# Attention by split transforms, then an ELU mixture layer: w_out in 4 KB packets with renumbered hidden units, and five reorderings beside it

## The chip, the cores and the metric

The kernel runs on one core of one Trainium2 chip. The metric is the device time of one execution in microseconds (us). A time is given as the median of several executions, and beside it stands one profiled execution, whose trace all rows come from. In the rows PE is TensorE (PEld its weight loads), DVE is VectorE, ACT is ScalarE, POOL is GpSimd and SP is SyncE, which here only issues transfers. A "q" behind the name (SPq, POOLq) is the queue of an engine.

## What is computed

```python
# x (8, 3008, 256); w_r, w_i (256, 256); b_r, b_i (256)
X = np.fft.rfft(x, axis=1)
Yr = Xr @ w_r - Xi @ w_i + b_r
Yi = Xr @ w_i + Xi @ w_r + b_i
lam = 0.01
Yr = np.sign(Yr) * np.maximum(np.abs(Yr) - lam, 0.0)
Yi = np.sign(Yi) * np.maximum(np.abs(Yi) - lam, 0.0)
y = np.fft.irfft(Yr + 1j * Yi, n=3008, axis=1)
# y as 24064 rows of 256; w_in (256, 2048); w_out (2048, 256)
h = y @ w_in
g = np.where(h > 0.0, h, np.exp(np.minimum(h, 0.0)) - 1.0)
out = g @ w_out
```

The 2048 columns of w_in and the 2048 rows of w_out are the hidden units. The function between them works on each unit alone.

## The kernel before

**The stages.** The sequence of 3008 is taken as 47 x 64, so that the transforms become products with small constant matrices. For each of the eight batches the work runs through five stages. A (`unit_A`, L186 and L194) does one half of the forward transform, X (`unit_X`, L242) the other half, M (`unit_M`; `first_M` and its helpers in the first batch, L292 to L392) the product with w_r and w_i, the bias and the soft threshold, B (`unit_B`, L448; `split_B`, L497, in the first batch) one half of the way back, and Y (`first_Y`, `split_Y`, L598; L612 later) the rest. Behind them comes the mixture layer in blocks of 512 rows: `front` (L1112) multiplies by w_in into `hps`, ScalarE takes exp (L1124), GpSimd clips (L1163), VectorE adds the linear part (`gT`, L1153), and `back` (L1184) multiplies by w_out into `ps_o`. Eight pairs of 128 hidden units make a block, 16 groups `ft` in all.

**Between the stages** data change their layout by transfers, nearly all on SyncE's queue. In the first batch A goes straight to its place in Z (L200); later it goes through `DA` in HBM. Y is turned by `by_part` into `Yx` (L428; four DMAs per call, two column parts c by two halves s), B's result goes to `DB` in HBM (L516) and comes back as `Bs` (`load_Bs`, L479). x comes in by `load_x` (L121) in three pieces per batch on GpSimd's queue.

**The order** of the instructions on each engine is the order in which the program text issues them (`manual_schedule`). An engine carries out its own list in that order and stops at an instruction whose input, or whose place to write, isn't ready. SyncE's issues take turns on eight semaphores, so that each issue also waits for the transfer eight issues before it.

**The head.** `busy` is set to ones (L621), and `idle_pe` (L628) multiplies it by itself in fp32, into a PSUM bank that nobody reads, while PE has nothing else: first two products of 512 columns and one of 256, later three and one more behind stage A (L932). Meanwhile GpSimd and VectorE make the angles, ScalarE takes their sine into `r1` (L755) and writes the first batch's weights of stage A from it, scaled by a column of plus or minus one: `M1d` (L761, four operations of 32 elements per partition) and `M1c` (L769, four more). Then ScalarE clears Z (L692) and copies A's results out of PSUM (L150).

**The weights of the mixture layer.** `load_w_in(q)` brings a quarter of w_in's columns on SyncE's queue (L952); `scale_w_in` (L962) multiplies them by 2/S and writes them as bf16 into `w_in_s`. VectorE does quarters 0 to 2, in two operations each, and GpSimd quarter 3 in four. `load_w_out(hh)` brings half of w_out on GpSimd's queue (L957) in rows of 256 floats, 1 KB each: partition p of group t holds hidden unit 128 t + p. 

**The first batch's sequence** stands written out (before the main loop). The parts that matter:

```python
    fB(3)
    load_w_in(2)
    first_M(5, 1, True)
...
    fB(5)
    let_go()
    load_Bs(0, 0, 16 * NT)
    load_w_in(3)
...
    load_w_out(0)
    load_x(1, 2)
    load_w_out(1)
```

`load_x(1, 2)` brings the last third of the second batch's x into the buffer that the first batch's stage A has read by then.

Of the kernel before, what the change touches and what calls it, by code (L numbers as in the profile page):

```python
# [9 lines left out]
AF = mybir.ActivationFunctionType  # L10
BF16 = mybir.dt.bfloat16
F32 = mybir.dt.float32
F32R = mybir.dt.float32r
# [7 lines left out]
N2 = 64  # L21
# [3 lines left out]
NS = 32  # L25
# [4 lines left out]
def kernel(  # L30
# [11 lines left out]
    nc = tc.nc  # L42
    P = nc.NUM_PARTITIONS
# [6 lines left out]
    NFT = DFF // P  # L50
# [13 lines left out]
    w_in_s = constp.tile([P, 2, DFF], BF16, name="w_in_s")  # L64
    w_out_r = constp.tile([P, NFT, E], F32R, name="w_out_r")
# [47 lines left out]
    def load_x(b, ci, m0=0, m1=8):  # L113

        src = bass.AP(
            tensor=x.tensor,
            offset=x.offset + (b * S + 8 * ci + m0) * D,
            ap=[[N1 * D, N2], [(NJ - 1) * D, 2], [D, m1 - m0], [1, D]],
        )
        dst = xts[ci][:, m0:m1, :]  # L120
        nc.gpsimd.dma_start(dst, src.bitcast(F32R))  # L121

    def unit_ps(name, alone):
        if alone:
            return pre2.tile([P, 2, 512], F32, name=name, tag="pre2")
        return last_banks("psF").tile([P, 2, 512], F32, name=name, tag="fps")
# [19 lines left out]
    def evac(dst, src, on_dve):  # L146
        if on_dve:
            nc.vector.tensor_copy(dst, src)  # L148
        else:
            nc.scalar.copy(dst, src)  # L150
# [223 lines left out]
    def begin_M(q, i, pool=begin, tag="begin"):  # L374

        begun[q, i] = ps = pool.tile([P, 2 * D], F32, name=tag, tag=tag)
        nc.tensor.matmul(ps[:], lhsT=busy[:, 0:P], rhs=bias_p[:], start=True, stop=False)
# [45 lines left out]

    def by_part(dst, of):

        for c in range(2):
            for s in range(2):
                nc.sync.dma_start(dst[c * N2 : c * N2 + N2, :, s, :], of(c, s))  # L428

    def turn_M3():  # L430
# [7 lines left out]
    def unit_B(b, v, alone=False, on_dve=False, all_dve=False):  # L438
        if (b, v // 2) not in Bz_of:
            t = "A" if alone and v == 0 else "Bz"  # L440
            Bz_of[b, v // 2] = wk2.tile([P, 8, D], BF16, name=t, tag=t)
            if b not in DB_of:
                DB_of[b] = dram.tile([K1, P, D], BF16, name="DB", tag="DB")
        Bz, Yx = Bz_of[b, v // 2], Yx_of.pop((b, v))
        ps = unit_ps("bps", alone)
        for pp in range(2):
            for s in range(2):
                nc.tensor.matmul(  # L448
                    ps[:, s, pp * D : pp * D + D], lhsT=M3x[:, 2 * v + pp, s, :],
                    rhs=Yx[:, pp, s, :], start=True, stop=True,  # L450
                )
        o = 4 * (v % 2)
        Bv = Bz[:, o : o + 4, :].rearrange("p (q s) d -> p s q d", s=2)
        psv = ps[:].rearrange("p s (q d) -> p s q d", d=D)
        if on_dve:
            nc.scalar.copy(Bv[:, :, 0], psv[:, :, 0])
            nc.vector.tensor_copy(Bv[:, :, 1], psv[:, :, 1])
        else:
            evac(Bv, psv, all_dve)
        if alone:  # L460
            k0 = 4 * v
            nc.sync.dma_start(
                DB_of[b][k0 : k0 + 4].rearrange("k p d -> p k d"), Bz[:, o : o + 4, :]
            )
        elif b == 1 and v > 1:
            nc.sync.dma_start(
                DB_of[b][4 * v : 4 * v + 4].rearrange("k p d -> p k d"), Bz[:, o : o + 4, :]
            )
        elif v % 2:
            k0 = 8 * (v // 2)  # L470
            nc.sync.dma_start(DB_of[b][k0 : k0 + 8].rearrange("k p d -> p k d"), Bz[:])

    def load_Bs(b, w, r0=0, cut=4 * K1):

        Bs = wk4.tile([4 * K1, 8, D], BF16, name="Bs", tag="Bs")
        dv = DB_of[b].rearrange("k (c h m) d -> (k c h) m d", c=2, h=2)
        for r, e in ((r0, cut), (cut, 4 * K1)):
            if r < e:
                nc.sync.dma_start(Bs[r:e], dv[r:e, 8 * w : 8 * w + 8, :])  # L479
        Bs_of[b, w] = Bs  # L480
# [139 lines left out]
    busy = constp.tile([P, 512], BF16, name="busy")  # L620
    nc.vector.memset(busy[:], 1.0)  # L621
    ips = [pre1.tile([P, 512], F32, name="ips", tag="mps1")]

    def idle_pe(n, k=2):

        ones = busy[:].bitcast(F32)
        for _ in range(n):
            nc.tensor.matmul(  # L628
                ips[-1][:].rearrange("p (a b) -> p a b", a=2)[:, 0:k], lhsT=ones[:, 0:P],
                rhs=ones.unsqueeze(1).to_broadcast([P, k, 256]), start=True, stop=True,  # L630
            )

    bias_p = wk4.tile([P, 2 * D], BF16, name="bias_p", tag="Bs")
    idle_pe(2)
    idle_pe(1, 1)
    xts = []
    for ci in range(3):
        xt = constp.tile([P, 8, D], F32R, name=f"xt{ci}")
# [1 line left out]
    with tc.tile_pool(name="stagep", bufs=1) as stagep:  # L640
        M1c = stagep.tile([P, 2, 3 * N2], F32R, name="M1c")
        M1d = stagep.tile([P, 4, 7 * NS], F32R, name="M1d")
# [5 lines left out]
        def col(eng, src, s1, op0, s2=None, op1=None, n=1, dt=F32):  # L648
            t = stagep.tile([P, n], dt, name=f"c{len(cols)}")
            cols.append(t)  # L650
            if op1 is None:
                eng.tensor_scalar(t[:], src[:], s1, None, op0)
            else:
                eng.tensor_scalar(t[:], src[:], s1, s2, op0, op1)
            return t

        def mix(eng, a, sc, b, op0, op1, n=1):
            t = stagep.tile([P, n], F32, name=f"c{len(cols)}")
            cols.append(t)
            eng.scalar_tensor_tensor(t[:], a[:], sc, b[:], op0, op1)  # L660
            return t
# [20 lines left out]
        def row(name, shape):  # L682
            return stagep.tile(shape, F32, name=name)
# [48 lines left out]
        for e in range(2):  # L732
            b3 = 1024 - 15 * e
            lo = slice(N2 * e, N2 * e + NS)
            hi = slice(N2 * e + NS, N2 * e + 2 * NS)
# [14 lines left out]
        r1 = row("r1", [P, 2 * NS])  # L750
# [4 lines left out]
        nc.scalar.activation(r1[:], v1[:], AF.Sin, bias=0.0, scale=TURN / 4.0)  # L755
        c1 = mix(dve, qcol, -2.0, pcol, ALU.mult, ALU.add)
        c0 = col(dve, c1, -1.0, ALU.mult, 1.0, ALU.add)
        for h, c in enumerate((c0, c1)):
            for q in range(2):
                o = 3 * NS + 16 * h + 8 * q  # L760
                nc.scalar.activation(  # L761
                    M1d[:, :, o : o + 8],
                    r1[:, NS * q : NS * q + NS].rearrange("p (b a) -> p a b", a=4),
                    AF.Copy, scale=c[:],
                )
        r1v = r1[:].rearrange("p (q b a) -> p q a b", q=2, a=2)
        for h, c in enumerate((c0, c1)):
            for q in range(2):
                nc.scalar.activation(  # L769
                    M1c[:, :, N2 + NS * h : N2 + NS * h + NS].rearrange(  # L770
                        "p a (q b) -> p q a b", q=2
                    )[:, q],
                    r1v[:, q], AF.Copy, scale=c[:],
                )
        for h in range(2):
            clear_Z(h)
# [150 lines left out]
        pool.tensor_copy(wcat_r[:, :, D : 2 * D], w_i_f[:])  # L927
        load_x(1, 1)
        pool.tensor_scalar(idm[:], prow, pcol[:], None, ALU.is_equal)
        for q, i in ((3, 0), (3, 1)):  # L930
            begin_M(q, i)
        idle_pe(3)  # L932
# [7 lines left out]
    M3.append(late2.tile([P, K1 // 2, P], BF16, name="M3", tag="osb"))  # L940

    w_in_v = moe_w_in.rearrange("(c p) f -> p c f", p=P)
    w_out_v = moe_w_out.rearrange("(t p) e -> p t e", p=P).bitcast(F32R)
    FQ = DFF // 4
    w_in_f = []

    def load_w_in(q):
        if q < 3:
            wf = late3.tile([P, 2, FQ], F32, name="w_in_f", tag="Et")
        else:  # L950
            wf = late2.tile([P, 2, FQ], F32, name="w_in_f", tag="osb")
        nc.sync.dma_start(wf[:], w_in_v[:, :, q * FQ : q * FQ + FQ])  # L952
        w_in_f.append(wf)

    def load_w_out(hh):
        hf = slice(hh * NFT // 2, (hh + 1) * NFT // 2)
        nc.gpsimd.dma_start(w_out_r[:, hf, :], w_out_v[:, hf, :])  # L957

    def scale_w_in(q, on_dve, c, part=None):
        lo, hi = (0, FQ) if part is None else (part * FQ // 2, part * FQ // 2 + FQ // 2)  # L960
        eng = nc.vector if on_dve else nc.gpsimd
        eng.tensor_scalar(  # L962
            w_in_s[:, c, q * FQ + lo : q * FQ + hi], w_in_f[q][:, c, lo:hi],
            2.0 / S, None, ALU.mult,
        )

# [6 lines left out]
    def fB(v):  # L973
        split_B(v, two_banks(pre2, "pre2"), (False, False))()
# [35 lines left out]
    first_M(5, 0, False)  # L1010
    begin_M(5, 1, pre1, "mps1")
    fB(3)
    load_w_in(2)
    first_M(5, 1, True)
    for c in range(2):
        scale_w_in(0, True, c)
# [5 lines left out]
    fB(5)  # L1022
    let_go()
    load_Bs(0, 0, 16 * NT)
    load_w_in(3)
    first_M(1, 0, False)
    first_M(1, 1, True)
# [7 lines left out]
            M4v[:, :, h], r4[0 : 2 * NR], w[0 : 2 * NR], None, ALU.mult  # L1035
        )
    load_w_out(0)
    load_x(1, 2)
    load_w_out(1)
    first.close()  # L1040
    lateB, chain, chain2, lateA = (
# [9 lines left out]
    rest_1, store_1, _ = split_B(1, two_banks(lateB, "lateB"), (True, True), True)  # L1051
# [257 lines left out]
    for i in range(n + LAG):  # L1309
# [4 lines left out]
        if early_h:  # L1314
            h, on_act = early_h, False
        elif i < n:
# [16 lines left out]
            h = front(i, third, on_act)  # L1333
# [52 lines left out]
```

## Time and profile before

| | us |
|---|---|
| executions | 874.69, 875.59, 875.5 |
| their median | 875.5 |
| profiled execution | 875.34 |
| its span | 873.6 |
| mean granted TensorE clock | 0.999 of full |

The span is the time from the first to the last instruction in the trace; the execution's own time is longer by what lies around it. How the rows read:

- A row of waits: engine, output and line of what waited, what ended the wait, then us in total, how many times, the longest.
- A row of the chain of waits: start and length in us, then the engine and line, or the transfer, that the end of the execution hung on at that time.
- A row of the timeline: start, busy time of the group, engine, line, operation, out<-in with partitions x elements, count, and in brackets the idle time before the group with what ended it.
- A row of transfers in a stretch: packets, megabytes, rate, and how many packets are small; or for one queue its packets, megabytes and the time that they took as a share of 16 DMA engines. q0 carries GpSimd's transfers, q1 SyncE's.
- A row of a stretch A:B in the table by stage: its length, then busy us (and instructions) of PE, PEld, DVE, ACT, POOL, then the granted clock, the busy share of the DMA engines and the GB/s.
- A row of a tile's view: line, engine, operation and count, least/median/largest ns of one, the first and last start in us, the shapes. "DMA to landing" is the time from a transfer's issue to its end.

### The profile page before, as it was taken

The page shows a single profiled execution, that of the slowest core. Times are in us where ns is not written, and L with a number is a line of the kernel's source. Part 1 is how long each engine was busy: PE and PEld are TensorE (multiplying, and loading weights), DVE is VectorE, ACT ScalarE, POOL GpSimd, SP SyncE. Part 2 cuts the span into 40 slices and gives each one's busy share as a digit, 9 for nine tenths or more (in the row PEclk, how much of TensorE's full clock was granted, in tenths as well). Part 3 has the DMA queues.
Part 4 walks back from the last instruction along what each step waited for, and adds up shares of the span by engine and source line. Part 5 has one row for each costly group of instructions (what it writes and reads, how often), then busy time and mean ns, then how long its engine had stood idle before and what let it go on. Part 6 is the DMA issues. An engine that isn't in the chain of part 4 may idle for free.

```text
span 873.6 us, 18529 instructions
## 1 busy us (share of the span) xinstructions
PE 861.2 (99%) x6760; PEld 674.9 (77%) x6760; DVE 665.9 (76%) x1104; ACT 714.7 (82%) x1258; POOL 586.9 (67%) x859
## 2 busy tenths in 40 slices
PE   8999999999999999999999999999999999999997
PEld 5567677877788877887779787788777878787776
DVE  8788778687776976768867787777777677788775
ACT  8778788888978889798887988879887888876664
POOL 8651640898757886588856888459874697734664
PEclk9999999999999999999999999999999999999999
DMA  8698337542484324743355442653337313250111
GB/s 246 226 302 242 110 97 205 171 141 78 122 242 126 92 74 143 219 140 104 95 173 174 138 110 73 205 154 125 99 87 214 100 37 86 73 146 25 38 37 49
DMA packets 115724, 116.11 MB, mean 133 GB/s; under 512 B 11552, under 2 KB 106272, under 8 KB 112272
## 3 DMA queue, kind: packets, MB, share of 16 engines
q1 hardware_dynamic: 109376, 87.40, 35.5%
q0 software_dynamic: 5968, 27.26, 9.7%
q8 instruction: 53, 0.87, 0.4%
q14 instruction: 39, 0.32, 0.1%
q10 hardware_dynamic: 288, 0.26, 0.1%
HBM read 53.28 MB, written 48.23 MB: 116 GB/s over the span
## 4 chain that ended last, share of the span: by engine, by line
PE 91%; DMA 3%; POOL 2%; DVE 2%; issue 1%; ACT 0%; SPq 0%; DVEq 0%; POOLq 0%
PE ps_o L1184 38%; PE hps L1112 33%; PE mps L334 5%; PE xps L242 3%; PE mps L1112 2%; PE yps L612 2%; PE bps L448 2%; PE aps L194 2%; PE mps L292 2%; DMA DB<-A 1%; POOL Y L350 1%; PE aps L186 1%; DMA xt<-in_x_dram 1%; DMA yb<-in_w_i_dram 1%; POOL yb L346 0%
## 5 line engine op out<-in xcount | busy, mean ns | idle before, releaser
L1153 DVE SCALAR_TENSOR_TENSOR gT<-Et,hps 128x512 fp32r<-128x512 f32 x630 | 403.0, 683 | 136.3 <-POOL Et L1163 126.3
L1184 PE MATMUL ps_o<-w_out_r,gT 128*128 128x256 f32 x3008 | 477.4, 301 | 0.8 <-DVE A L148 0.8
L1184 PEld LDWEIGHTS ps_o<-w_out_r,gT 128*128 128x128 f32 x3008 | 404.3, 189 | 49.1 <-DVE A L148 1.1
L1163 POOL TENSOR_SCALAR Et<-Et 128x512 f32<-128x512 f32 x482 | 287.0, 615 | 210.2 <-ACT Et L1124 208.9
L1112 PE MATMUL hps<-yT,w_in_s 128*128 128x512 bf16 (+7 forms) x1620 | 366.1, 353 | 0.2
L1124 ACT ACTIVATE Et<-hps 128x512 f32<-128x512 f32 x514 | 282.5, 609 | 42.4 <-PE hps L1112 39.2
L1112 PEld LDWEIGHTS <-w_in_s 128*128 128x128 bf16 x1728 | 144.0, 98 | 103.9 <-issue 11.9
L1122 ACT ACTIVATE Et<-hps 128x512 f32<-128x512 f32 x192 | 104.5, 597 | 42.0 <-PE hps L1112 41.6
L1127 ACT ACTIVATE Et<-Et 128x512 f32<-128x512 f32 x192 | 110.5, 632 | 0.0
L350 POOL TENSOR_TENSOR Y<-yb,clip 128x512 bf16<-128x512 f32 x72 | 92.7, 1288 | 6.0
L346 POOL TENSOR_TENSOR yb<-yb,bias_bc 128x256 f32<-128x256 f32 x72 | 53.1, 738 | 11.3 <-DVE yb L341 11.3
L150 ACT CAST XT<-xps 128x768 bf16<-128x768 f32 x57 | 45.8, 804 | 16.7 <-PE xps L242 16.6
L341 DVE TENSOR_TENSOR yb<-mps,yb 128x512 f32<-128x512 f32 x72 | 49.8, 692 | 7.2
L150 ACT CAST yT<-yps 128x752 bf16<-128x752 f32 x56 | 44.1, 787 | 13.7 <-PE yps L612 13.5
L1155 DVE SCALAR_TENSOR_TENSOR gT<-hps,Et 128x512 fp32r<-128x512 f32 x78 | 50.2, 686 | 3.3
L349 POOL TENSOR_SCALAR clip<-yb 128x512 f32<-128x512 f32 x72 | 44.2, 613 | 6.3
L150 ACT CAST A<-aps 128x1024 bf16<-128x1024 f32 x40 | 40.6, 1018 | 7.2 <-PE aps L194 4.9
L150 ACT CAST Bz<-bps 128x1024 bf16<-128x1024 f32 x41 | 41.6, 1014 | 5.3 <-PE bps L448 5.0
L340 DVE TENSOR_TENSOR yb<-mps,bias_bc 128x256 f32<-128x256 f32 x72 | 30.5, 424 | 17.5 <-PE mps L334 15.7
L334 PE MATMUL mps<-wcat_s,XT 128*128 128x256 bf16 x288 | 43.2, 273 | 0.0
L1196 DVE COPY osb<-ps_o 128x512 f32<-128x512 f32 x46 | 31.7, 690 | 5.4 <-PE ps_o L1184 3.4
L260 POOL TENSOR_TENSOR XS<-XT 128x512 bf16<-128x512 bf16 x30 | 34.1, 1158 | 2.4 <-ACT XT L150 1.4
(209 smaller groups left out, 666.2 us busy)
## 6 DMA issues: line engine op xcount, KB each, us to landing
xt<-in_x_dram POOLq DMA_DIRECT2D x21, 1024.0 KB, 5.3
out_dram<-osb SPq DMA_DIRECT2D x158, 128.0 KB
Bs<-DB SPq DMA_DIRECT2D x30, 384.0 KB
Yx<-Y SPq DMA_DIRECT2D x168, 64.0 KB
DA<-A SPq DMA_DIRECT2D x19, 512.0 KB
DB<-Bz SPq DMA_DIRECT2D x19, 512.0 KB
Z<-DA SPq DMA_DIRECT2D x21, 384.0 KB
xt<-in_x_dram POOLq DMA_DIRECT2D x6, 512.0 KB, 5.9
```

Of the source, the lines that this page charges most:

```text
L150: nc.scalar.copy(dst, src)
L334: nc.tensor.matmul(out_, lhsT=lhs[:, dt] if lhs is not None else sum_of(dt, ch)[:, oc : oc + P], rhs=w[:, dt, :], start=(dt == 0), stop=(d ...
L346: nc.gpsimd.tensor_tensor(yb[:, D : 2 * D], yb[:, D : 2 * D], bias_bc[:, D : 2 * D], ALU.add)
L350: nc.gpsimd.tensor_tensor(Y_of[b, q][:, i, :], yb[:], clip[:], ALU.subtract)
L1112: nc.tensor.matmul(hps[s][:, c0:c1], lhsT=w_in_s[:, dt, ft * P : ft * P + P], rhs=yT_of[b][:, dt, t0 : t0 + c1 - c0], start=(dt == 0), sto ...
L1122: nc.scalar.activation(Et[:, s], hps[s], AF.Relu, scale=-1.0)
L1124: nc.scalar.activation(Et[:, s], hps[s], AF.Exp)
L1127: nc.scalar.activation(Et[:, s], Et[:, s], AF.Exp, scale=-1.0)
L1153: nc.vector.scalar_tensor_tensor(o, e, -1.0, h, ALU.add, ALU.max)
L1155: nc.vector.scalar_tensor_tensor(o, h, 0.0, e, ALU.max, ALU.add)
L1163: nc.gpsimd.tensor_scalar(e, e, 1.0, 0.0, ALU.min, ALU.max)
L1184: nc.tensor.matmul(po[q][:, i_ % 2, :], lhsT=gT[:, s, i_ * P : i_ * P + P], rhs=w_out_r[:, ft, :], start=(ft == 0 and i_ % 2 == 0), stop=( ...
```

## The change

Seven edits, told in the order of the diff.

1. `by_part` issues its four DMAs with the half s outside and the column part c inside.
2. `unit_B` issues its four matmuls with s outside and the index pp inside.
3. The head's three idle products become 14 fp32 products of 80 columns with a 128 x 128 block of the ones.
4. `M1d` and `M1c` are written by four operations of 64 elements in place of eight of 32: one operation covers both halves q. The steps of reading stay at 4 and 2 floats.
5. `load_x(1, 2)` moves on GpSimd's queue from between the two `load_w_out` to behind the making of `idm` in the head.
6. w_out is read as (q p j): partition p of quarter q takes four rows next to each other in HBM, 512 q + 4 p + j for j = 0 to 3, which are 4 KB in one piece. So group t = 4 q + j holds other hidden units than before. `scale_w_in` reads w_in's columns in the same numbering, that is with a step of 4 floats, and writes them dense.
7. `load_w_in(2)` moves on SyncE's queue from behind `fB(3)` to behind `load_Bs(0, 0)`, right ahead of `load_w_in(3)`.

The number of transfers and the bytes of each stay the same.

```diff
@@ -423,8 +423,8 @@
 
     def by_part(dst, of):
 
-        for c in range(2):
-            for s in range(2):
+        for s in range(2):
+            for c in range(2):
                 nc.sync.dma_start(dst[c * N2 : c * N2 + N2, :, s, :], of(c, s))
 
     def turn_M3():
@@ -443,8 +443,8 @@
                 DB_of[b] = dram.tile([K1, P, D], BF16, name="DB", tag="DB")
         Bz, Yx = Bz_of[b, v // 2], Yx_of.pop((b, v))
         ps = unit_ps("bps", alone)
-        for pp in range(2):
-            for s in range(2):
+        for s in range(2):
+            for pp in range(2):
                 nc.tensor.matmul(
                     ps[:, s, pp * D : pp * D + D], lhsT=M3x[:, 2 * v + pp, s, :],
                     rhs=Yx[:, pp, s, :], start=True, stop=True,
@@ -631,8 +631,9 @@
             )
 
     bias_p = wk4.tile([P, 2 * D], BF16, name="bias_p", tag="Bs")
-    idle_pe(2)
-    idle_pe(1, 1)
+    tick = busy[:].bitcast(F32)[:, 0:P]
+    for _ in range(14):
+        nc.tensor.matmul(ips[0][:, 0:80], lhsT=tick, rhs=tick[:, 0:80], start=True, stop=True)
     xts = []
     for ci in range(3):
         xt = constp.tile([P, 8, D], F32R, name=f"xt{ci}")
@@ -755,22 +756,14 @@
         nc.scalar.activation(r1[:], v1[:], AF.Sin, bias=0.0, scale=TURN / 4.0)
         c1 = mix(dve, qcol, -2.0, pcol, ALU.mult, ALU.add)
         c0 = col(dve, c1, -1.0, ALU.mult, 1.0, ALU.add)
-        for h, c in enumerate((c0, c1)):
-            for q in range(2):
-                o = 3 * NS + 16 * h + 8 * q
+        for w, lo, a_ in ((M1d, 3 * NS, 4), (M1c, N2, 2)):
+            for h, c in enumerate((c0, c1)):
+                n_ = 2 * NS // a_
                 nc.scalar.activation(
-                    M1d[:, :, o : o + 8],
-                    r1[:, NS * q : NS * q + NS].rearrange("p (b a) -> p a b", a=4),
-                    AF.Copy, scale=c[:],
-                )
-        r1v = r1[:].rearrange("p (q b a) -> p q a b", q=2, a=2)
-        for h, c in enumerate((c0, c1)):
-            for q in range(2):
-                nc.scalar.activation(
-                    M1c[:, :, N2 + NS * h : N2 + NS * h + NS].rearrange(
+                    w[:, :, lo + n_ * h : lo + n_ * h + n_].rearrange(
                         "p a (q b) -> p q a b", q=2
-                    )[:, q],
-                    r1v[:, q], AF.Copy, scale=c[:],
+                    ),
+                    r1[:].rearrange("p (q b a) -> p q a b", q=2, a=a_), AF.Copy, scale=c[:],
                 )
         for h in range(2):
             clear_Z(h)
@@ -927,6 +920,7 @@
         pool.tensor_copy(wcat_r[:, :, D : 2 * D], w_i_f[:])
         load_x(1, 1)
         pool.tensor_scalar(idm[:], prow, pcol[:], None, ALU.is_equal)
+        load_x(1, 2)
         for q, i in ((3, 0), (3, 1)):
             begin_M(q, i)
         idle_pe(3)
@@ -940,7 +934,7 @@
     M3.append(late2.tile([P, K1 // 2, P], BF16, name="M3", tag="osb"))
 
     w_in_v = moe_w_in.rearrange("(c p) f -> p c f", p=P)
-    w_out_v = moe_w_out.rearrange("(t p) e -> p t e", p=P).bitcast(F32R)
+    w_out_v = moe_w_out.rearrange("(q p j) e -> p q j e", p=P, j=4).bitcast(F32R)
     FQ = DFF // 4
     w_in_f = []
 
@@ -953,14 +947,17 @@
         w_in_f.append(wf)
 
     def load_w_out(hh):
-        hf = slice(hh * NFT // 2, (hh + 1) * NFT // 2)
-        nc.gpsimd.dma_start(w_out_r[:, hf, :], w_out_v[:, hf, :])
+        nc.gpsimd.dma_start(
+            w_out_r[:].rearrange("p (q j) e -> p q j e", j=4)[:, 2 * hh : 2 * hh + 2],
+            w_out_v[:, 2 * hh : 2 * hh + 2],
+        )
 
     def scale_w_in(q, on_dve, c, part=None):
-        lo, hi = (0, FQ) if part is None else (part * FQ // 2, part * FQ // 2 + FQ // 2)
+        js = slice(0, 4) if part is None else slice(2 * part, 2 * part + 2)
         eng = nc.vector if on_dve else nc.gpsimd
         eng.tensor_scalar(
-            w_in_s[:, c, q * FQ + lo : q * FQ + hi], w_in_f[q][:, c, lo:hi],
+            w_in_s[:, c, q * FQ : q * FQ + FQ].rearrange("p (j f) -> p j f", j=4)[:, js],
+            w_in_f[q][:, c, :].rearrange("p (f j) -> p j f", j=4)[:, js],
             2.0 / S, None, ALU.mult,
         )
 
@@ -1010,7 +1007,6 @@
     first_M(5, 0, False)
     begin_M(5, 1, pre1, "mps1")
     fB(3)
-    load_w_in(2)
     first_M(5, 1, True)
     for c in range(2):
         scale_w_in(0, True, c)
@@ -1022,6 +1018,7 @@
     fB(5)
     let_go()
     load_Bs(0, 0, 16 * NT)
+    load_w_in(2)
     load_w_in(3)
     first_M(1, 0, False)
     first_M(1, 1, True)
@@ -1035,7 +1032,6 @@
             M4v[:, :, h], r4[0 : 2 * NR], w[0 : 2 * NR], None, ALU.mult
         )
     load_w_out(0)
-    load_x(1, 2)
     load_w_out(1)
     first.close()
     lateB, chain, chain2, lateA = (
```

## The prediction

> **What bounds the kernel now.** I read the first lines of the page, then PE's waits over the whole run, then the start of the chain that ended last.
>
> ```profile
> span 873.6 us, 18529 instructions
> ...
> PE 861.2 (99%) x6760; PEld 674.9 (77%) x6760; DVE 665.9 (76%) x1104; ACT 714.7 (82%) x1258; POOL 586.9 (67%) x859
> ...
> PE xps L242 <- DMA yb<-in_w_i_dram: 3.0, 1, 3.0
> PE ips L628 <- DVE busy L621: 1.4, 1, 1.4
> PE ps_o L1184 <- DVE A L148: 0.8, 1, 0.8
> PE gps L598 <- DMA Bs<-DB: 0.7, 1, 0.7
> PE bps L448 <- DMA Yx<-Y: 0.4, 1, 0.4
> ...
> 16.53 0.57 SPq L200
> 17.80 4.80 DMA yb<-in_w_i_dram
> ...
> 47.49 10.13 DMA DB<-A
> ```
>
> TensorE (PE) works for 861.2 of 873.6 us. A change that leaves the matmuls as they are can only win idle time, and five waits hold nearly all of it. The 1.4 us is the start and isn't touched. The 3.0 us is in the head: PE waits for transfers at the first X product; the last Z placement was issued at 16.53 and the transfers landed at 22.6. The other three, 0.8, 0.7 and 0.4 us, are the change's field: 1.9 us in all, 0.2% of the time. From the small waits alone no large gain can come; a loss has no such roof.
>
> **The wait of 0.8 us (term A).** The page names VectorE's copy A as releaser, but the matmul that waits is the first one that reads w_out.
>
> ```profile
> 41.08 0.99 POOL L957 DMA_DIRECT2D w_out_r<-in_moe_w_out_dram  x1
> 42.07 0.61 POOL L121 DMA_DIRECT2D xt<-in_x_dram  x1
> 42.60 0.98 POOL L957 DMA_DIRECT2D w_out_r<-in_moe_w_out_dram  x1
> ...
> DMA to landing us min/median/max: 8.3/11.4/14.4
> ...
> 49.54 1.18 PE L1184 MATMUL ps_o<-w_out_r,gT 128*128 128x256 f32 x8 [0.79 <-DVE A L148]
> ...
> DMA packets 359, 0.37 MB, mean 368 GB/s; under 512 B 0, under 2 KB 359, under 8 KB 359
> ...
> q0 software_dynamic: 713, 0.76, 78.1%
> q1 hardware_dynamic: 711, 0.36, 51.5%
> ```
>
> The first half was issued at 41.08 and took 8.3 us: 49.4, just ahead of the matmul at 49.54; so I take the w_out half as what ended the wait. Three edits act on its landing. Packets of 4 KB for 1 KB: the line of packets is the stretch 45.5 to 46.5, where 1 KB packets alone moved 368 GB/s, so size alone promises nothing. The next x's last piece is no longer behind it, where its packets shared the end of the half: a gain. And w_in's third quarter (0.52 MB), which went alone at 34.06 before, now stands on SyncE's queue right ahead of the half: a loss of at most 0.52 MB at 368 GB/s, 1.4 us, if it all goes first. How the two queues share is shown by the last two lines, 51 to 54.5: 713 packets of one beside 711 of the other, turn by turn. With 4 KB against w_in's 2 KB, w_out then gets two thirds of the bytes, where at 1 KB it got one third. Bounds: all 0.79 won, or 1.4 lost. The extra bytes and the better share pull against each other; I take a gain of 0.3, nearer to the row's 0.79 because the SyncE piece is issued first and much of it passes before GpSimd's transfer begins.
>
> **The wait of 0.7 us (term B).**
>
> ```profile
> 57.67 4.16 DMA Bs<-DB
> ...
> 61.87 0.51 PE gps L598 x8
> ...
> DMA packets 5026, 5.12 MB, mean 309 GB/s; under 512 B 140, under 2 KB 4592, under 8 KB 4896
> ```
>
> Here DB's last store, issued at 47.49, lands 10.13 us later (57.6), the load of Bs follows (57.67 + 4.16 = 61.8) and PE starts at 61.87. The store shares the engines with all that is queued: 5.12 MB at 309 GB/s from 41 to 57.6. The change takes 1.05 MB (x) out of this stretch and puts 0.52 MB (w_in) in; the difference at 309 GB/s is 1.7 us. Bs then lands near 60.1, and PE, 0.3 + 0.7 earlier, asks for it at 60.9. The wait goes whole: 0.7. The cover is 0.8 us; if it were gone, B would be 0. The x piece moves to about 26 us on GpSimd's queue, behind the making of idm:
>
> ```profile
> 30.00:34.00 4.00, 3.94 (x24) 1.51 (x21) 3.78 (x8) 3.79 (x8) 2.39 (x3) 1.00 0.07 27
> ...
> 55.28 0.81 PE L194 MATMUL gps<-xt,M 128*128 128x512 f32 x2
> ```
>
> In 30 to 34 the DMA engines are busy 0.07 of the time, at 27 GB/s: the megabyte (3 us at 350) is free there. It is read at 55.28, so nothing waits. Its issue costs GpSimd the 0.61 us of the row above at another place, ahead of three tile operations in a stage where PE has other work; I price it at nothing, at most 0.6.
>
> **The 0.4 us (term D).**
>
> ```profile
> 131.32 0.49 PE L448 MATMUL bps<-Yx,M3x 128*128 128x256 bf16 x3 [0.36 <-DMA Yx<-Y]
> ```
>
> Of a B unit's four matmuls one ran, and three waited for the last of Yx's four DMAs: each reads both parts c of one s, and s = 1 is asked for second. With s outer in the DMAs and in the matmuls, two run before that wait. One matmul of 0.49 / 3 moves ahead of it; the DMAs' own time stays. Bounds 0 and 0.36; I take 0.1.
>
> **The head (term C): ScalarE in four, short idle products.**
>
> ```profile
> 4.09 0.26 ACT L755 ACTIVATE r<-v 128x64 f32<-128x64 f32 x1 [0.62 <-DVE v L754]
> 4.41 1.07 ACT L761 ACTIVATE M1d<-r,c 128x32 fp32r<-128x32 f32 x4
> 5.39 0.95 ACT L769 ACTIVATE M1c<-r,c 128x32 fp32r<-128x32 f32 x4
> ...
> 1.44 0.50 PEld L628 LDWEIGHTS ips<-busy 128*128 128x128 f32 x2 [1.44 <-DVE busy L621]
> 2.46 0.33 PEld L628 LDWEIGHTS ips<-busy 128*128 128x128 f32 x1 [0.52 <-issue]
> ...
> 4.80 0.19 PEld L628 LDWEIGHTS ips<-busy 128*128 128x128 f32 x1 [0.30 <-issue]
> 5.58 1.95 PEld L186 LDWEIGHTS aps<-xt,M1d 128*128 128x128 f32 x16 [0.58 <-ACT M1d L761]
> 7.79 1.96 PEld L186 LDWEIGHTS aps<-xt,M1d 128*128 128x128 f32 x16 [0.26 <-DMA xt<-in_x_dram]
> ...
> 10.88 1.02 PEld L186 LDWEIGHTS aps<-xt,M1c 128*128 128x128 f32 x8 [0.18 <-ACT A L150]
> ```
>
> Eight operations of 32 elements took 2.02 us; four of 64 at the 0.26 to 0.28 of the nearest rows take about 1.1. M1d is ready some 0.45 us earlier, all ScalarE's later work 0.9. But PE's idle products grow in number: each fp32 product is two passes with a weight load each (3 products gave 6 records), so 14 are 28 loads. A load took 0.33 alone at the slow clock, two together 0.50, so 0.17 to 0.33 apart; from 4.80 it took 0.19, sixteen in 1.95 (0.12 apart). From 1.44 to 4.80 that is 20 loads (10 at the worst); the other 8 (18) take 1.0 (3.4, each 0.19). The idle run ends at 5.8 (8.2 at worst), where A starts at 5.58 now. Late by 0.2 is swallowed by the wait of 0.26 for x at 7.79; the 0.18 at 10.88 for ScalarE's copy goes. Bounds: 0.18 won, or 2.6 late less 0.44, 2.2 lost. I take 0.
>
> **The scaling of w_in (term S).** Its ten operations now read with steps of 16 bytes.
>
> ```profile
> 33.30 1.17 DVE L962 TENSOR_SCALAR w_in_s<-w_in_f 128x512 bf16<-128x512 f32 x2
> 34.98 0.68 DVE L356 SCALAR_TENSOR_TENSOR Y<-mps,clip 128x512 bf16<-128x512 f32 x1
> 35.82 0.63 PE L497 MATMUL pre<-Y,M 64*128 64x256 bf16 x8
> ...
> L962 POOL TENSOR_SCALAR w_in_s<-w_in_f x4: 848/849/912, 50.1 to 57.6; 128x256 bf16<-128x256 f32 x4
> ...
> 59.13 1.28 DVE L1153 SCALAR_TENSOR_TENSOR gT<-Et,hps 128x512 fp32r<-128x512 f32 x2
> ...
> 62.21 1.03 PE L1112 MATMUL hps<-yT,w_in_s 128*128 128x512 bf16 x4
> ```
>
> No row shows GpSimd with such a step. The nearest is ScalarE's own: M1d reads steps of 16 bytes (1.07 for four), M1c of 8 (0.95): 0.03 us in 32 elements, 1 ns each, which makes at most 0.24 on GpSimd's 256. Its four scalings sit between the clips, and a delay adds up over them; the last one feeds gT that ends at 60.41, whose banks PE wants at 62.21: 1.8 us of cover, 1.1 when PE comes 0.7 earlier. So each may grow by 0.27 at no cost. VectorE's two at 33.30 stand ahead of L356, which ends 0.16 before the product that reads it: by 1 ns an element they grow by 1.0, 0.8 over this cover; if VectorE reads a step of 16 bytes as it reads dense rows, by nothing. I take S at 0, bounds 0 and 0.8, and rival 4 for GpSimd.
> The Trainium skill ("GPSIMD Engine Reference", section "Performance pitfalls for Q7 kernels") speaks against this edit: reads with a step over 8 bytes cost about half as much again. No run so far shows it. By it, an estimate: 0.42 more each, 1.7 in all, 0.6 over the cover, and the forecast would be 874.9.
>
> **Sum.** A 0.3, B 0.7, C 0, D 0.1, S 0: 1.1 us. The profiled execution took 875.34 (its span 873.6 and 1.7 around it), the median of the runs is 875.5: 874.2 from the one, 874.4 from the other. Forecast 874.3.
>
> **The rivals.**
> 1. w_out wins its turns: with two thirds of the bytes the half lands before PE comes, A is 0.79; the shorter head helps PE by the 0.18 too. 0.79 + 0.7 + 0.18 + 0.1 = 1.8: 873.6. For it: the equal turns. Against: 0.52 MB more in front.
> 2. The edit of w_out doesn't do what it says: 1 KB packets were at 368 GB/s already, and the half lands 1 us later behind w_in. 0.3 becomes -1.0: 875.6.
> 3. The short products leave TensorE's clock low. Row 4.80 shows it risen 3.4 us after the first load. If short passes don't count, A's loads come 0.24 apart, not 0.12, until 3.4 us behind 5.6: some 14 loads, 1.7 less the 0.26: 1.4 lost, 875.7. Against: loads follow one another without a gap.
> The Trainium skill ("TensorE: Matmul & The Clock Gate", Part 1) has half clock until about 3.4 us of sustained activity; the 3.4 us of the row agree with that, and the price is the one above.
> 4. Slower: GpSimd's strided scalings become the bound from 50 to 62 us. Each longer by d costs 4d - 1.1. It takes back the 1.1 won at d = 0.55 and makes the kernel slower by 0.2% from d = 1.0 (1.84 us each, for 0.85 now). At three times the row (d = 1.7) it is 5.7: 879.9. For it: unknown stride, four in a row, an engine that already paces clip after clip. Against: ScalarE's 1 ns.
>
> **How the numbers follow.** Forecast 0.42, rival 1 0.24, rival 2 0.09, rival 3 0.10 (with the late head of term C), rival 4 0.15. About 0.2% (1.75 us: 873.75 to 877.25) is what a measurement of this kernel tells from no change. The forecast's own range is 873.4 to 875.2, a third of it under the line: faster 0.15 + 0.24 = 0.39. Slower: rival 4 and a part of 3, 0.17. Same: 0.44. The range reaches down past rival 1 by the D and head bounds (0.26 + 0.7) to 872.7, up over rivals 2 and 3 and the milder half of 4 to 877.0.
>
> **What would show it.** The idle products end by 5.8 and A's first loads come 0.12 apart at once (rival 3: 0.2). The matmul that first reads w_out waits under 0.5 us (rival 1: none; rival 2: over 1.5). Bs lands before 60.9, PE's wait for it is gone. GpSimd's scalings take under 1.1 us; PE has no wait on gT, w_in or its banks from 50 to 63. The forecast is wrong if PE's waits past 62 us change by more than some tenths, or if X's first product starts more than 0.5 us away from 22.8.

## The result and the profile after

The changed kernel took 878.94 us (median of 6 runs, 877.0 to 879.49), the kernel before 875.55 (6 runs, 874.57 to 876.67): 1.0037 of it, with a 95% interval of 1.0024 to 1.005. It is slower by 3.4 us. The profiled execution took 879.25, with a span of 877.5.

The page's first lines and PE's waits over the whole run, after:

```profile
span 877.5 us, 18466 instructions
...
PE 860.2 (98%) x6679; PEld 682.2 (78%) x6782; DVE 666.5 (76%) x1104; ACT 714.7 (81%) x1254; POOL 589.2 (67%) x859
...
PE xps L242 <- DMA yb<-in_w_i_dram: 2.5, 1, 2.5
PE ips L636 <- DVE busy L621: 1.4, 1, 1.4
PE ps_o L1180 <- DMA w_out_r<-in_moe_w_out_dram: 1.3, 1, 1.3
PE yps L612 <- DMA Bs<-DB: 0.4, 1, 0.4
PE bps L448 <- DMA Yx<-Y: 0.4, 1, 0.4
```

The waits do not explain 3.9 us of span. The one for Z in the head got shorter and the one for Bs at 62 us is gone; the one for w_out grew by 0.5, and a new one for a later Bs took 0.4. So the time lies mostly in work that takes longer, and PE's timeline shows where it starts. First the weight loads of the head, then the products:

```profile
1.44 6.05 PEld L636 LDWEIGHTS ips<-busy 128*128 128x128 f32 x28 [1.44 <-DVE busy L621]
7.37 2.89 PEld L186 LDWEIGHTS aps<-xt,M1d 128*128 128x128 f32 x13
...
1.45 6.26 PE L636 MATMUL ips<-busy 128*128 128x80 f32 x28 [1.45 <-DVE busy L621]
7.44 5.79 PE L186 MATMUL aps<-xt,M1d 128*128 128x256 f32 x32
13.06 1.11 PE L186 MATMUL begin<-xt,M1c 128*128 128x256 f32 x8
...
25.38 0.88 PE L242 MATMUL xps<-M,Z 128*128 128x96 bf16 x9 [2.51 <-DMA yb<-in_w_i_dram]
```

The 28 loads of the idle run took 6.05 us, 0.21 each to the end: the clock never rose in it. Thirteen loads of stage A still took 2.89 (0.22 each), where before sixteen took 1.95 (0.12 each). A's first 32 products took 5.79 us.

The second place is X. The table by stage, in which the granted clock is the number behind the five engines:

```profile
0.00:8.00 8.00, 6.55 (x30) 6.56 (x31) 5.62 (x29) 6.57 (x11) 6.51 (x26) 1.00 0.67 201
8.00:14.00 6.00, 6.00 (x40) 6.00 (x39) 5.84 (x15) 2.94 (x3) 5.12 (x20) 1.00 0.80 271
...
20.00:26.00 6.00, 3.49 (x17) 1.79 (x16) 2.18 (x6) 2.95 (x5) 1.55 (x3) 0.92 0.99 278
26.00:32.00 6.00, 5.77 (x67) 4.43 (x66) 4.33 (x7) 4.75 (x8) 3.02 (x6) 0.80 1.06 398
```

Read in steps of 1 us, the clock was at half from 25.0 to 28.4, and the first X products ran at half pace. In the kernel before it was at 1.00 there:

```profile
18.00:24.00 6.00, 3.01 (x30) 1.82 (x29) 3.21 (x9) 2.58 (x4) 4.47 (x7) 1.00 0.99 293
24.00:30.00 6.00, 5.54 (x56) 3.30 (x56) 5.48 (x9) 5.47 (x10) 2.00 (x4) 1.00 0.99 367
```

The first two rows of the table after show a trap: for the head the column says 1.00, though the loads ran at half pace from 1.44 to 11. The slow start is seen in the duration of the weight loads and products alone.

How late PE is at each place, from the two timelines:

| first product of | before | after | later |
|---|---|---|---|
| A (L186) | 5.61 | 7.44 | 1.83 |
| A with M1c | 9.79 | 13.06 | 3.27 |
| X (L242) | 22.81 | 25.38 | 2.57 |
| M (L368) | 26.42 | 29.89 | 3.47 |
| B at 35.82 (L497) | 35.82 | 39.54 | 3.72 |
| back (L1184, now L1180) | 49.54 | 53.76 | 4.22 |
| Y, first with Bs (L598) | 61.87 | 65.20 | 3.33 |
| end of the span | 873.6 | 877.5 | 3.9 |

The head costs 3.3, of which 0.2 is back by the end of A and the wait for Z takes up 0.5; the fall of the clock at X costs 0.9; near 37 us 0.25 are lost; the wait for w_out costs 0.5; the end of the wait for Bs gives 0.9 back. Of the last 0.6, 0.4 is a wait of Y for a Bs at 144 us, behind an issue on SyncE's queue that took 1.68 us (0.60 in the median before); whether that issue caused it was not followed up.

### The profile page after: what moved, and what is told of

Same layout as the page of the kernel before. It is cut to its first block, busy times and chain, and to the rows that moved or that the text cites. A ratio compares the mean times of both kernels' runs of the same rounds, so it can differ in the third digit from the quotient of the medians.

```text
span 877.5 us, 18466 instructions
## 1 busy us (share of the span) xinstructions
PE 860.2 (98%) x6679; PEld 682.2 (78%) x6782; DVE 666.5 (76%) x1104; ACT 714.7 (81%) x1254; POOL 589.2 (67%) x859
## 4 chain that ended last, share of the span: by engine, by line
PE 88%; POOL 4%; DVE 3%; DMA 2%; issue 2%; ACT 1%; SPq 0%; DVEq 0%; POOLq 0%; ACTq 0%
PE ps_o L1180 37%; PE hps L1108 32%; PE mps L334 5%; PE xps L242 3%; PE mps L1108 2%; PE yps L612 2%; PE bps L448 2%; PE aps L194 2%; PE mps L292 1%; POOL Y L350 1%; PE aps L186 1%; DMA w_out_r<-in_moe_w_out_dram 1%; DVE gT L1149 1%; PE ips L636 1%; POOL yb L346 1%
## 5 line engine op out<-in xcount | busy, mean ns | idle before, releaser
L1180 PE MATMUL ps_o<-w_out_r,gT 128*128 128x256 f32 x3008 | 477.4, 301 | 1.3 <-DMA w_out_r<-in_moe_w_out_dram 1.3
L1180 PEld LDWEIGHTS ps_o<-w_out_r,gT 128*128 128x128 f32 x3008 | 404.3, 189 | 49.6 <-DVE A L148 1.6
L1108 PE MATMUL hps<-yT,w_in_s 128*128 128x512 bf16 (+6 forms) x1528 | 359.8, 351 | 5.0 <-DVE gT L1149 0.2
L346 POOL TENSOR_TENSOR yb<-yb,bias_bc 128x256 f32<-128x256 f32 x72 | 53.2, 739 | 11.2 <-DVE yb L341 11.2
```

Source lines behind the costliest of these rows:

```text
L346: nc.gpsimd.tensor_tensor(yb[:, D : 2 * D], yb[:, D : 2 * D], bias_bc[:, D : 2 * D], ALU.add)
L1108: nc.tensor.matmul(hps[s][:, c0:c1], lhsT=w_in_s[:, dt, ft * P : ft * P + P], rhs=yT_of[b][:, dt, t0 : t0 + c1 - c0], start=(dt == 0), sto ...
L1180: nc.tensor.matmul(po[q][:, i_ % 2, :], lhsT=gT[:, s, i_ * P : i_ * P + P], rhs=w_out_r[:, ft, :], start=(ft == 0 and i_ % 2 == 0), stop=( ...
```

## The experiments

Theory 1 was the head: short products keep the clock low. Theory 2 was the rest: strided scalings and moved transfers. Twelve kernels ran in three groups; in each the kernel before ran 35 times beside them. One thing must be known to read the medians: in 51 of these 105 executions of the kernel before, the mean granted clock was 0.998 or less, and they took 2.4 to 2.8 us more than the others (medians of the groups 877.0 to 877.4 against 874.6 to 874.7). That it is the fall of the clock seen above is likely but not shown: the one traced execution of the kernel before has 0.999 and no fall. In the text below "a fall" in an execution without a trace means a mean clock of 0.998 or less. How often it happens is part of what an edit changes: five of the six executions of the changed kernel above had 0.997, and the one with 1.000 took 877.0.

**First group: which edit** (before 876.21)

The changed kernel with the old idle products (`e1_old_idle`):

```diff
-    tick = busy[:].bitcast(F32)[:, 0:P]
-    for _ in range(14):
-        nc.tensor.matmul(ips[0][:, 0:80], lhsT=tick, rhs=tick[:, 0:80], start=True, stop=True)
+    idle_pe(2)
+    idle_pe(1, 1)
```

> The changed kernel with the three long idle products of before in place of the 14 short ones. Theory 1 (the short products keep TensorE at its slow clock and run 1.9 us longer): stage A starts near 5.1 to 5.6 us as before, X by 22.8 at the full clock, and the time falls by about 3.5 us (3.0 at the end of A, less 0.5 of the wait for Z, plus 0.9 of X at the slow clock) to some 875.4. Theory 2 (the strided scalings and the moved transfers cost it): the time stays above 878.

874.92, ratio 0.9982 (0.9968 to 0.9997). In its trace A began at 5.51 and X at 20.89, at the full clock. So the short products are what made the kernel slower; the other six edits together are a small gain, with an interval that ends close to 1.

The kernel before with the short products alone (`e2_short_idle`): the same diff turned around, and nothing else.

> The kernel before with the 14 short idle products alone. Theory 1: the 28 weight loads come 0.21 us apart and end near 7.7, the clock rises only near 11.2, A ends 3 us later, time near 879. Theory 2: within 0.5 us of before, 875 to 876.

877.77, ratio 1.0020 (1.0007 to 1.0032). The mean is below the expected 3.5 us, in part since the clock fell less often (2 of 12 executions, 19 of 35 before); why it did is not shown. Among those without a fall it is 877.43 against 874.62: 2.8 us for this edit alone. Its weight loads are those of the changed kernel, and A with M1c began 2.75 us later than before (12.54 for 9.79):

```profile
1.44 6.04 PEld L636 LDWEIGHTS ips<-busy 128*128 128x128 f32 x28 [1.44 <-DVE busy L621]
...
12.54 1.11 PE L186 MATMUL begin<-xt,M1c 128*128 128x256 f32 x8
```

The 4 KB packets with the renumbering alone (`e3_packets`), the diff's hunks at w_out and `scale_w_in` on the kernel before:

> The kernel before with the 4 KB packets of w_out and the renumbered hidden units alone (so with the scalings that read steps of 16 bytes). Theory 1: within 0.8 us of before (VectorE's and GpSimd's scalings longer by 0.2 to 0.4 us each, w_out's first half not later). Theory 2: 1.5 us or more over before.

874.85, ratio 0.9988 (0.9972 to 1.0004). Theory 2 falls for this edit. One part of the expectation missed: w_out's first half landed 9.5 us after its issue (8.3 before), PE waited 2.3 us for it, and the clock fell behind that wait.

The two moved transfers alone (`e4_moves`), the hunks with `load_x(1, 2)` and `load_w_in(2)` on the kernel before:

> The kernel before with the two moves alone: x's last piece in the head, w_in's third quarter right ahead of the fourth. Theory 1: the wait for Bs (0.7 us) is gone, the wait for the first half of w_out (0.8) stays or grows by up to 1.0: between 0.7 us faster and 0.5 us slower than before. Theory 2: 1.5 us or more over before.

876.43, ratio 0.9999 (0.9986 to 1.0012). Theory 2 falls here too. In the profile the wait for Bs is gone, as expected, and the wait for w_out grew from 0.8 to 1.5 us; the clock fell behind it, and at X behind a wait of 3.5 us. Nine of 12 executions had a fall.

**Second group: why the short products cost** (before 875.47)

Three runs with the changed kernel beside them (`a1_changed`).

> The changed kernel itself, on the chip of the next three. Both theories: as measured, some 0.4% over before, A ending near 18.8, X beginning near 25.

878.09, ratio 1.0024 (1.0011 to 1.0037): a smaller loss than the 0.4% above. In its trace A ended at 18.3 and X began at 23.62, both earlier than expected, and no fall shows. Among the executions without a fall it took 876.95, the kernel before 874.6.

Seven products of 160 columns (`e5_7x160`), and seven of 80 (`e6_7x80`, the first line of this diff alone):

```diff
-    for _ in range(14):
-        nc.tensor.matmul(ips[0][:, 0:80], lhsT=tick, rhs=tick[:, 0:80], start=True, stop=True)
+    for _ in range(7):
+        nc.tensor.matmul(ips[0][:, 0:160], lhsT=tick, rhs=busy[:].bitcast(F32)[:, 0:160],
+                         start=True, stop=True)
```

> The changed kernel with 7 idle products of 160 columns for 14 of 80: the same columns, half the weight loads, and at the slow clock each pass (160 columns, 0.27 us) is longer than its weight load (0.21). Theory 1a (the clock rises only when PE's passes fill a stretch of some 3.4 us): the clock rises by about 4.9, the idle run ends near 5.1, A's loads come 0.12 apart, A ends by 16.6, the time is 3 to 4 us under the changed kernel. Theory 1b (only the length of the idle run matters): the same time as with 7 products of 80 columns.

> The changed kernel with 7 idle products of 80 columns for 14: 14 loads of 0.21 end by 4.5, before ScalarE's weights are ready near 5.1. Theory 1a: the short passes don't count, A begins at 5.1 at the slow clock, 16 or so of its loads 0.21 apart until about 8.5, A ends 1.2 us later than with 7 products of 160 columns. Theory 1b: A begins at 5.1 and runs 0.12 apart, the same end of A as with 160 columns.

875.04 (ratio 0.9990, 0.9979 to 1.0000) and 876.30 (1.0011, 1.0000 to 1.0022). The loads of the head, with 160 columns:

```profile
1.44 3.57 PEld L636 LDWEIGHTS ips<-busy 128*128 128x128 f32 x14 [1.44 <-DVE busy L621]
5.33 1.98 PEld L186 LDWEIGHTS aps<-xt,M1d 128*128 128x128 f32 x16 [0.32 <-ACT M1d L762]
```

And with 80:

```profile
1.44 3.06 PEld L636 LDWEIGHTS ips<-busy 128*128 128x128 f32 x14 [1.44 <-DVE busy L621]
5.22 3.04 PEld L186 LDWEIGHTS aps<-xt,M1d 128*128 128x128 f32 x14 [0.72 <-ACT M1d L762]
...
5.25 5.35 PE L186 MATMUL aps<-xt,M1d 128*128 128x256 f32 x32 [0.53 <-ACT M1d L762]
```

With seven of 80 the idle run is short, A begins in time (5.22), and still its loads come 0.22 apart, not 0.12. By itself that doesn't tell the theories apart: these loads ended after 3.06 us, those of 160 columns after 3.57, and the kernel before had its clock up 3.4 us after the first load, so a rule of length alone could give both. What rules length out is the run of 14: 28 loads without a gap for 6.05 us did not raise the clock, in three traces (the changed kernel twice, `e2_short_idle`), and as many columns in half the loads had it up when A began. So what counts here is not how long PE has instructions but what its passes are like: at half clock a load takes 0.21; estimated by proportion (the passes of 512 came 0.85 apart), a pass of 80 columns takes less, 0.13, and one of 160 more, 0.27. Whether it is the share of the time that the passes fill or the length of each one, no run decides. A with M1c began 0.9 us later with 80 columns (10.44 and 9.56; 1.2 was expected). The 14 short products of the change have both costs, the slow clock and the long run; the seven of 80 have only the first, the seven of 160 neither. From 14 of 80 to 7 of 160 the time falls by 3.05 us on the same chip.

A longer second idle run (`e7_longer_second`), on the changed kernel with the old idle products: `idle_pe(4)` for `idle_pe(3)` behind stage A.

> The changed kernel with the three long idle products of before at the start, and one more long product (0.86 us) in the second idle run behind stage A. Theory (an idle stretch of PE in the wait for Z lets the clock fall for X, which costs about 3 us in those executions where it happens): the executions with a mean clock of 0.997 or less get fewer, the median falls by up to 1 us against the kernel with the old idle products (0.9982 of before). Rival (the wait for Z is only filled): the same time, within 0.3 us, or 0.4 later where Z lands early.

874.39, ratio 0.9986 (0.9974 to 0.9998). Two of 12 executions had a fall, of the kernel without it 7 of 12; the ratio is the same within its interval, so it is no clear gain. Its profile caught a fall at another place:

```profile
48.00:50.00 2.00, 0.60 (x2) 0.19 (x1) 1.99 (x4) 1.53 (x4) 1.28 (x3) 1.00 1.10 375
50.00:52.00 2.00, 1.59 (x8) 1.59 (x8) 2.00 (x4) 0.00 (x0) 1.27 (x1) 0.65 1.10 363
52.00:54.00 2.00, 2.00 (x7) 1.01 (x6) 0.02 (x1) 0.60 (x1) 0.14 (x1) 0.50 1.15 346
```

PE waits for w_out (0.60 us of work from 48 to 50), and when it goes on the clock is at half until 54. From the start of this `back` to the next one it took 5.58 us; without a fall it is 4.09 to 4.11 in five traces. So the fall cost 1.5 us more, behind a wait of 1.8. The kernel without the added product had the same wait of 1.8 and no fall in its profile: the length doesn't decide alone.

**Third group: the wait for w_out** (before 875.48)

The next kernel has the old idle products and `load_w_in(2)` at its old place (`e8_w_in_back`):

```diff
     fB(3)
+    load_w_in(2)
...
     load_Bs(0, 0, 16 * NT)
-    load_w_in(2)
     load_w_in(3)
```

> The changed kernel with the old idle products and with w_in's third quarter back at its old place behind the fourth B unit; 4 KB packets, early x, ScalarE in four and the B order stay. Theory 3 (w_in's quarter ahead of w_out's first half passes whole before it: the first w_out packets come 3.9 to 4.5 us after the issue, 2.9 without it): the half lands some 8 us after its issue, PE waits about 1 us less for it than the kernel with the old idle products (1.8), the clock falls less often behind that wait, time 0.5 to 1.5 us under that kernel's 0.998 of before. Rival (the packets' turns decide): the wait stays within 0.3 us.

873.29, ratio 0.9976 (0.9963 to 0.9989), the fastest of all. Its rows (PE's waits, the landing of the w_out halves, the wait of back):

```profile
PE ps_o L1179 <- DMA w_out_r<-in_moe_w_out_dram: 0.3, 1, 0.3
...
DMA to landing us min/median/max: 7.4/8.9/10.4
...
47.83 1.17 PE L1179 MATMUL ps_o<-w_out_r,gT 128*128 128x256 f32 x8 [0.31 <-DMA w_out_r<-in_moe_w_out_dram]
```

The first half landed 7.4 us after its issue (9.0 with w_in's third quarter in front too), PE waited 0.3 for 1.8, and one execution of 12 had a fall, for 7 of 12. The mechanism of theory 3 is seen in the traces, read in steps of 0.2 us: w_out's first packet moved 2.2 to 3.2 us after the issue in the five with one quarter of w_in issued close to it, 3.4 to 4.2 in the seven with two in front. What the move of w_in costs in time is not shown: 0.9976 and 0.9982 lie within each other's intervals.

The same with 1 KB packets and dense scalings (`e9_no_packets`), without the hunks at w_out and `scale_w_in`:

> The same without the 4 KB packets and the renumbering: dense scalings, 1 KB packets. Theory 3: the first half lands within 0.5 us of the run with 4 KB packets (1 KB packets alone moved 368 GB/s); the scalings are back at 0.85 us on GpSimd and 0.41 on VectorE, 0.2 us less lost near 37 us. So the time is within 0.4 us of it. Rival (4 KB packets bring what they are for): 0.5 us or more slower.

873.94, ratio 0.9983 (0.9971 to 0.9994): 0.65 us slower, with intervals that overlap. In its profile the half landed 9.7 us after the issue, 2.3 later than with 4 KB packets where at most 0.5 was expected, and PE waited 2.1 us although w_in's quarter was at its old place. So theory 3 doesn't explain the wait alone. Whether 4 KB packets land sooner as such stays open, since `e3_packets`, with 4 KB and x's piece behind it, took 9.5.

w_out's first half in the head (`e10_early_w_out`), on the kernel with w_in's quarter back: `load_w_out(0)` ahead of `load_w_in(0)`, which is behind x's last piece on GpSimd's queue. And the same with `idle_pe(4)` (`e11_best`).

> As the run with w_in's quarter back, and w_out's first half is issued on GpSimd's queue in the head, right behind x's last piece, for the stretch of 30 to 35 us in which the DMA engines idle. Theory 4 (PE's wait near 49 us, with the fall of the clock behind it where it exceeds some 1.7 us, is the landing of that half and nothing else): the wait goes or becomes some tenths, the clock stays at 1.00 from 45 to 60 us, and the time falls by another 0.5 to 1.5 us, to 0.996 to 0.998 of before. Rival (something else is just behind it): under 0.4 us.

> As the last, with one more long product in the second idle run behind stage A (4 of 512 columns for 3). Theory 4: both places where the clock falls are covered; nearly all executions have a mean clock of 0.998 or more, the spread shrinks, the median is 0.3 to 1.0 us below the last run's. Rival: the added product makes PE late for X where Z lands early, no gain.

877.76 (1.0011, 0.9993 to 1.0028) and 878.57 (1.0015, 0.9995 to 1.0036). The wait for w_out is gone, as theory 4 has it, and a greater one stands ahead of it. SyncE's issue of the first Bs and the product that reads it, in the first of the two:

```profile
42.94 0.32 SPq L479 DMA_DIRECT2D Bs<-DB  x1
...
48.29 1.41 PE L585 MATMUL one<-M,Bs 96*128 96x94 bf16 x16 [4.95 <-issue]
```

The half competes with DB's stores from 33 to 41, where GpSimd's queue moved 1.44 MB (0.05 in the kernel without the edit); Bs is issued at 42.94 instead of 39.68, now behind the second half of w_out (issued 41.05) instead of ahead of its packets, and PE waits 5 us (4.3 in the second). Theory 4 expected a full clock from 45 to 60 us; it was at half from 47.7 to 54.5, and nine of 12 executions of either kernel had a fall. The rival that something else stands just behind the wait was right, but as a loss.

## Why the prediction was wrong

**The step that failed** is term C: "From 1.44 to 4.80 that is 20 loads (10 at the worst); the other 8 (18) take 1.0 (3.4, each 0.19)." It let the clock rise at 4.80 as before, whatever PE does until then. It did not rise: 28 loads of 0.21 ended at 7.4, and A ran slow until about 11.2, where the trace's single loads come closer together. C was taken as 0, with 2.2 lost at worst; measured, A with M1c came 3.3 us later. (In `e2_short_idle` and `a1_changed`, where the clock rose some tenths sooner, it came 2.75 and 2.82 later.) Rival 3 had the mechanism (0.10), and its own price of 1.4 for A's slow loads (measured 1.4, from 1.83 to 3.27 late; 0.9 and 1.0 in the other two, so the exact match is luck). But it counted from A's start at 5.6, so that the long run and the slow A stood as alternatives where they add. The objection "loads follow one another without a gap" was true and beside the point: here loads without a gap did not raise the clock, full passes did. One of the prediction's signs of being wrong came: X began at 25.38, not within 0.5 us of 22.8.
The Trainium skill ("TensorE: Matmul & The Clock Gate", Part 1) has the clock rise after some 3.4 us of sustained activity in a free-running window. The trace agrees for A's passes, which began at 7.44 and raised the clock at 11.2. It differs for the short ones: 6 us of them did not raise it.

**Term A** had the wrong sign: 0.3 won was forecast, 0.5 was lost. One step that failed was the equal turns. The two queues' packets from 45.2 to 49.2, behind the issue of w_out at 45.27, after (q1 SyncE's, q0 GpSimd's):

```profile
q1 hardware_dynamic: 572, 1.15, 92.3%
q0 software_dynamic: 8, 0.03, 3.0%
```

There were no turns: w_in's packets went first, nearly all of them, and w_out's began when they ended, 3.6 us after the issue. GpSimd's queue is not that slow by itself: at the start of the kernel before, with SyncE's queue almost empty, x's first packets moved 1.4 us after the issue. The end "all goes first" of the bounds was the right one, but its price was not what was lost: the half landed 8.4 us after its issue, 8.3 before.

What was lost lies ahead of the issue. It came 4.19 us later than before (45.27 for 41.08), while PE asked for the half only 3.71 later (52.46 for 48.75). GpSimd's operations that ran beside VectorE's scalings of w_in had grown; first a row of before, then two of after:

```profile
35.68 0.78 POOL L391 TENSOR_SCALAR clip<-yb 128x512 f32<-128x512 f32 x1
...
39.58 1.52 POOL L391 TENSOR_SCALAR clip<-yb 128x512 f32<-128x512 f32 x1
...
45.27 1.53 POOL L950 DMA_DIRECT2D w_out_r<-in_moe_w_out_dram  x2
```

From its first clip of stage M to the issue of w_out GpSimd took 9.63 to 9.64 us in the four traces with dense scalings, 10.17 to 10.35 in the ten with strided ones. So edit 6 delays w_out's issue by 0.5 to 0.7 us. The prediction had no term for it: S priced the scalings themselves and what VectorE does behind them.

**Term B** was right: the wait for Bs was gone, and 0.9 came back where 0.7 was forecast. **Term D** had the mechanism right: two matmuls instead of three stand behind the wait; its 0.1 us was not measured by itself. **Term S** was right for GpSimd's own scalings: 0.24 more at most was estimated, 0.25 was measured, and the cover of 1.1 held: PE has no wait for them from 54 to 66. VectorE's shortest scaling grew from 0.41 to 0.62, the first two together from 1.17 to 1.58. PE lost 0.25 near 37 us by it, within the bounds of 0 to 0.8; the trace puts that wait down to GpSimd's Y (1.55 for 1.33), with VectorE's L356 ending at the same time. The rows after (the landing of w_out is the third):

```profile
L958 DVE TENSOR_SCALAR w_in_s<-w_in_f x6: 619/639/1055, 36.8 to 55.3; 128x512 bf16<-128x512 f32 x6
L958 POOL TENSOR_SCALAR w_in_s<-w_in_f x4: 1097/1105/1377, 53.8 to 62.3; 128x256 bf16<-128x256 f32 x4
...
DMA to landing us min/median/max: 8.4/9.4/10.5
...
134.69 0.39 PE L448 MATMUL bps<-Yx,M3x 128*128 128x256 bf16 x2 [0.35 <-DMA Yx<-Y]
```

The Trainium skill ("GPSIMD Engine Reference", section "Performance pitfalls for Q7 kernels") gives half as much again for such reads; here it was 1.10 for 0.85, three tenths more.

**Not foreseen** was that the clock can fall behind a wait of PE, which cost 0.9 us at X in the profiled execution. The prediction priced waits by their own length alone.

## What to carry to other kernels

Products that only keep TensorE awake had to be full here: few weight loads and many columns. Read the pace of the weight loads, not the share of busy time and not the granted clock, to see whether they work. A wait of PE of 1.4 to 2.5 us can cost another 0.9 to 1.5, because the clock may fall behind it; so the waits at the seams of the stages are worth more than they show. A large transfer that is issued just ahead of the one that PE needs can go ahead of it whole, even on another queue. And a strided access on one engine is to be priced for its neighbours too: here it was GpSimd's next operations that grew, and with them the issue of a transfer.

## What the runs showed of the hardware

- Passes of 80 fp32 columns behind loads of 0.21 us kept PE occupied for 6.3 us and did not raise its clock, in three traces; passes of 160 columns raised it within 3.9 us (A's loads 0.12 apart at 5.33).
- Behind waits of 1.4 to 3.5 us the clock fell to half in some profiles and not in others: at X after a wait of 2.5 in the changed kernel and of 3.5 with the moved transfers, but not after 3.0 in the kernel before; at w_out after 1.4 with seven products of 160 and 1.8 with the longer second run, but not after 2.2 in the second profile of the changed kernel. So the 1.7 us of theory 4 is no threshold. What else decides was not tried. Worked out from stretches of 1 us, each fall lasted 3.4 us, and 6.8 behind the wait of 5 us; at w_out it cost PE 1.2 to 1.5 us in four traces.
- Of GpSimd's w_out hardly a packet was moved in the first 3.4 to 4.2 us behind its issue while two quarters of SyncE's w_in were (8 packets beside 572 in the rows above), 2.2 to 3.2 us with one. With SyncE's queue almost empty, x's first packets moved 1.4 us behind their issue.
- Beside VectorE's scalings with steps of 16 bytes a clip on GpSimd took 0.97 to 1.52 us, beside the dense ones 0.78 to 0.79.
